# Split expert weights kept in DRAM after the first of three passes, sums kept in PSUM, and a later start for a float64 conversion

## The chip, the cores and the metric

The kernel runs on one core of one Trainium2 chip. The metric is the device time of one execution in microseconds (us), given as the median of several runs. All reading below is from one profiled execution and its trace. TensorE is PE in the profile, VectorE is DVE, ScalarE is ACT, GpSimd is POOL and SyncE is SP.

## What is computed

Three stages in a row. A delta-rule attention over 768 steps makes x (3072 tokens, 384 wide). A mixture of eight experts with Sinkhorn-balanced gates P takes x. A gated linear block with weights of type float64 takes that result.

```python
def _moe_ref(x, w_gate, w1, w2):
    P = ...                                # 8 Sinkhorn rounds on exp(x @ w_gate)
    for e in range(8):
        h = np.maximum(x @ w1[e], 0.0)     # 384 -> 1024
        out += P[:, e:e + 1] * (h @ w2[e])  # 1024 -> 384
    return out

def _moe2_ref(x, w1, w2, w3, w_out):
    h = (x @ w1) * (x @ w2) @ w3
    return h @ w_out
```

## The kernel before

Every float32 matrix product is made of three matmuls: an operand is split into a part `hi` that TensorE takes as it is and the rest `lo`, and hi·hi, hi·lo and lo·hi are summed. Splitting costs one ACT copy (`hi`) and one subtraction on POOL or DVE (`lo`).

The program is a list of operations with dependencies, priorities and estimated costs (`Plan`). Its `order` method plays them through once in the kernel's own estimates and writes out a fixed order for each engine. On the chip each engine then works through its own list strictly in that order, waiting on semaphores. An operation that is late therefore holds up all that stand behind it on its engine.

Three stretches follow each other. Up to about 530 us of the span: attention, the gates and expert 0. From there to about 1960 us, phase B: experts 1 to 7. To the end, phase C: the gated block. Phase B is 42 **units**: three passes over the tokens (two blocks of 512 in each, `PASSES`), in each pass seven experts, in each expert two halves `h` of the hidden width. A unit has 138 matmuls of 512 columns. Its first layer has 66: for each of two column **pairs** `q` (256 hidden units each), seven steps over three PSUM banks X, Y and Z, in a Strassen-like scheme with eleven block products instead of twelve or more, on sums of blocks of x (`forms`, made at each pass's start) and on sums of blocks of w1 (`wS`). Its second layer has 72 (`m2`): six sums of twelve matmuls, each read out by DVE into `tmp`, times P, and added to `acc` by POOL.

- **Weights, `load_pair`.** For each pair, four SP DMAs bring raw w1 and w2 blocks into the two `rawB` buffers. ACT copies and POOL (or DVE) subtractions make hi and lo in `wA`, five small sums on POOL or DVE make the Strassen combinations, and more copies and subtractions make `wS`. This is done for every unit, in all three passes anew, though the weights are the same. `wA` and `wS` hold two units: the weights of unit n+1 go where those of unit n-1 were, which is free when unit n-1's second layer has been read.
- **Sums, `hold` and `done`.** In steps 0, 2 and 3 of a pair ACT copies a bank to one of four SBUF buffers `rt` (`hold`). TensorE's next product into that bank waits for the copy. In steps 1, 4 and 5 `done` adds another bank to that buffer (DVE), ACT makes ReLU of it as hi, DVE makes lo; the `rt` buffer is free after the last of the three.
- **Conversion, `convert`.** The gated block's weights come as float64. 72 jobs on one buffer each (`cvr`, `cv`) turn them into hi and lo by integer operations: five DVE, two ACT and three POOL-or-DVE operations, a load and two stores on SP. They have the lowest priority and may begin when the buffers of phase B are open.
- **`add_first`.** Once in each pass, at expert 4, the result of expert 0 is read from DRAM, scaled and added. It takes two of the four `rt` buffers and both `tmp` buffers meanwhile.

Of the kernel before, what the change touches and what calls it, by code (L numbers as in the profile page):

```python
# [6 lines left out]
F32 = mybir.dt.float32  # L7
# [14 lines left out]
NE = 8  # L22
# [20 lines left out]
BB = 2.0  # L43
NG12 = 1
# [265 lines left out]
class Kernel:  # L310
# [56 lines left out]
    def setup(self):  # L367
# [22 lines left out]
                  w3_d=((2, 128, 8, 1024), F32))  # L390
# [448 lines left out]
    def load_pair(self, e_, h, q, prio):  # L839
# [4 lines left out]
        ps = 2 * h + q  # L844
        raws = []
# [29 lines left out]
        for m, src, dst, key in ((256, lambda: T["rawB"][:, r1.at, 0:256], lambda i: ws(i), lambda i: ("wS", ps, i, 0)),  # L875
                                 (256, lambda: T["rawB"][:, r2.at, 0:256], lambda i: ws(i, 256), lambda i: ("wS", ps, i, 1)),
                                 (128, lambda: T["rawB"][:, r1.at, 256:384], lambda i: self.wb(n1 + 1)[:, 768 * i:768 * i + 128], lambda i: ("w", sl2, i))):
            g.op({"ACT": actb(m)}, lambda e, src=src, dst=dst: self.copy("ACT", dst(0), src()), r=rk + ["bopen"], w=[key(0)], prio=prio)
            g.op({"POOL": pool2(m), "DVE": BB * dveb(m, True)}, lambda e, src=src, dst=dst: self.tt(e, dst(1), src(), dst(0).bitcast(F32), ALU.subtract),
                 r=rk + [key(0)], w=[key(1)], prio=prio)  # L880

# [82 lines left out]
    def unit(self, p, e_, h, pr, pe, pb):  # L964
# [22 lines left out]
        def product(q, step, idx):  # L987
# [24 lines left out]
            def done(nm, s, out):  # L1012
                t = temps[q, nm]
                tv = lambda: T["rt"][:, t.at]
                hv = lambda i: self.hv(out)[:, i]
                g.op({"DVE": dveb(512)}, lambda e: self.tt("DVE", tv(), self.ps(s, 512), tv(), ALU.add), r=[s], w=[t], prio=pe)
                g.op({"ACT": actb(512)}, lambda e: nc.scalar.activation(out=hv(0), in_=tv(), func=AF.Relu), r=[t], w=[(out, 0, 0)], prio=pe)  # L1017
                g.op({"DVE": dveb(512, True)}, lambda e: self.stt(hv(1), tv(), 0.0, hv(0).bitcast(F32), ALU.max, ALU.subtract),
                     r=[t, (out, 0, 0)], w=[(out, 1, 0)], prio=pe)
            if step == 0:  # L1020
                hold("X1", X)
            elif step == 1:
                done("X1", Z, hq["11"])
            elif step == 2:
                hold("X2", X)
            elif step == 3:
                hold("Y1", Y)
            elif step == 4:
                done("Y1", X, hq["22"])
            elif step == 5:  # L1030
                done("X2", Y, hq["12"])
            else:
                out = hq["21"]
                hv = lambda i: self.hv(out)[:, i]
                g.op({"ACT": actb(512)}, lambda e: nc.scalar.activation(out=hv(0), in_=self.ps(X, 512), func=AF.Relu),
                     r=[X], w=[(out, 0, 0)], prio=pe)
                g.op({"DVE": dveb(512)}, lambda e: self.stt(hv(1), self.ps(X, 512), 0.0, hv(0).bitcast(F32), ALU.max, ALU.subtract),
                     r=[X, (out, 0, 0)], w=[(out, 1, 0)], prio=pe)
# [50 lines left out]
    def phase_b(self):  # L1089
# [30 lines left out]
        for n, (p, e_, h) in enumerate(units):  # L1120
            pr = 400.0 + n
            if n == 0:
                for q in range(2):
                    self.load_pair(e_, h, q, 390)
# [7 lines left out]
            if n + 1 < len(units):  # L1132
                for q in range(2):
                    self.load_pair(*units[n + 1][1:], q, pr + .5)
            self.unit(p, e_, h, pr, 250.0 + n / 100, pb)
            if (e_, h) == (4, 0):
# [36 lines left out]
    def convert(self):  # L1173
# [12 lines left out]
        for nm, src, kk, c0, m in jobs:  # L1186
# [5 lines left out]
                     m * 1024, ["bopen"], [raw], pr)  # L1192
# [248 lines left out]
```

## Time and profile before

| what | value |
|---|---|
| median of 3 runs | 2313.74 us (2311.77 to 2315.23) |
| the profiled execution's own time | 2319.72 us |
| its span, first to last instruction | 2318.0 us |
| mean granted TensorE clock in the span | 0.965 of full |
| busy share of PE, DVE, POOL, ACT | 93%, 62%, 53%, 36% |
| moved by DMA | 194.82 MB, mean 84 GB/s |

The profile gives for each engine the busy time, and for each stretch of the span the busy time and the number of instructions. Idle time of an engine is put down to the engine whose semaphore ended the wait. A granted clock below 1 means that TensorE ran below its full 2.4 GHz in part of the stretch.

### The profile page before, as it was taken

The page shows a single profiled execution, that of the slowest core. Times are in us where ns is not written, and L with a number is a line of the kernel's source. Part 1 is how long each engine was busy: PE and PEld are TensorE (multiplying, and loading weights), DVE is VectorE, ACT ScalarE, POOL GpSimd, SP SyncE. Part 2 cuts the span into 40 slices and gives each one's busy share as a digit, 9 for nine tenths or more (in the row PEclk, how much of TensorE's full clock was granted, in tenths as well). Part 3 has the DMA queues.
Part 4 walks back from the last instruction along what each step waited for, and adds up shares of the span by engine and source line. Part 5 has one row for each costly group of instructions (what it writes and reads, how often), then busy time and mean ns, then how long its engine had stood idle before and what let it go on. Part 6 is the DMA issues. An engine that isn't in the chain of part 4 may idle for free.

```text
span 2318.0 us, 40182 instructions
## 1 busy us (share of the span) xinstructions
PE 2153.9 (93%) x16017; PEld 1822.8 (79%) x16017; DVE 1436.1 (62%) x2037; ACT 843.5 (36%) x1664; POOL 1233.7 (53%) x1264
## 2 busy tenths in 40 slices
PE   2999999989999799989999799999999999999999
PEld 2899999987777677767777577788887788888888
DVE  7566765667878877777787786655555555222211
ACT  3333243334434343444443334433343333122222
POOL 3000000047887987787887897876678765300000
PEclk6989999999999999999999899999999999999999
DMA  5231232133233332243233332232222214700000
GB/s 187 87 100 39 81 91 59 31 107 118 94 123 103 105 96 85 84 127 110 84 98 104 110 96 73 64 105 64 64 67 70 64 60 154 145 28 28 14 14 28
DMA packets 200476, 194.82 MB, mean 84 GB/s; under 512 B 13984, under 2 KB 175712, under 8 KB 199520
## 3 DMA queue, kind: packets, MB, share of 16 engines
q1 hardware_dynamic: 182528, 174.43, 24.4%
q0 software_dynamic: 17760, 17.83, 3.0%
q8 instruction: 125, 2.05, 0.4%
q14 instruction: 63, 0.52, 0.1%
HBM read 156.98 MB, written 35.23 MB: 83 GB/s over the span
## 4 chain that ended last, share of the span: by engine, by line
PE 55%; POOL 14%; DVE 11%; DMA 9%; issue 6%; ACT 4%; SPq 1%; DVEq 0%; POOLq 0%; ACTq 0%
PE b L332 55%; DMA rawB<-in_moe_w 3%; POOL rawB L343 3%; POOL acc L343 3%; POOL cv L343 3%; POOL wA L343 2%; DVE cv L346 2%; POOL wS L343 2%; DMA w_d<-cv 2%; SPq L363 1%; DVE hB L346 1%; DVE cv L1199 1%; DVE tmp L343 1%; DMA xst<-xs_d 1%; ACT wA L336 1%
## 5 line engine op out<-in xcount | busy, mean ns | idle before, releaser
L332 PE MATMUL b<-hB,wA 128*128 128x512 f32 x2277 | 580.1, 395 | 1.5 <-DVE hB L346 1.4
L332 PEld LDWEIGHTS b<-hB,wA 128*128 128x128 f32 x2277 | 427.3, 188 | 105.7 <-DVE hB L346 3.1
L343 POOL TENSOR_TENSOR wA<-rawB,wA 128x768 fp32r<-128x768 f32 (+2 forms) x228 | 326.2, 1439 | 171.1 <-ACT wA L336 169.1
L343 POOL TENSOR_TENSOR acc<-acc,tmp 128x512 f32<-128x512 f32 x252 | 340.0, 1351 | 67.7 <-DVE tmp L343 65.4
L343 DVE TENSOR_TENSOR rt<-b,rt 128x512 f32<-128x512 f32 x300 | 204.0, 685 | 247.5 <-PE b L332 217.4
L332 PE MATMUL b<-xr,wA 128*128 128x256 f32 (+1 forms) x1620 | 327.6, 340 | 0.0
L332 PE MATMUL b<-hA,wA 128*128 128x256 f32 (+1 forms) x1611 | 326.0, 335 | 0.8 <-DVE hA L346 0.7
L332 PEld LDWEIGHTS b<-xr,wA 128*128 128x128 f32 x1620 | 256.5, 196 | 33.7 <-DVE rt L343 0.4
L332 PEld LDWEIGHTS b<-hA,wA 128*128 128x128 f32 x1611 | 247.5, 190 | 36.3 <-DVE hA L346 3.7
L332 PE MATMUL b<-xT,wA 128*128 128x512 f32 x1008 | 251.4, 390 | 1.5 <-POOL wA L343 1.2
L332 PE MATMUL b<-xT,wS 128*128 128x512 f32 x756 | 215.0, 410 | 32.9 <-ACT rt L336 25.0
L336 ACT ACTIVATE wA<-rawB 128x768 fp32r<-128x768 f32 (+2 forms) x252 | 157.8, 627 | 228.6 <-DMA rawB<-in_moe_w 166.8
L343 DVE TENSOR_TENSOR tmp<-b,pb 128x512 f32<-128x512 f32 x234 | 159.7, 683 | 123.1 <-PE b L332 111.7
L336 ACT ACTIVATE rt<-b 128x512 f32<-128x512 f32 x300 | 174.3, 592 | 149.1 <-PE b L332 107.7
L332 PEld LDWEIGHTS b<-xT,wA 128*128 128x128 f32 x1008 | 188.9, 188 | 43.2 <-POOL wA L343 1.8
L346 DVE SCALAR_TENSOR_TENSOR hB<-rt,hB 128x512 fp32r<-128x512 f32 x170 | 169.5, 1003 | 62.6 <-ACT hB L1017 60.8
L332 PEld LDWEIGHTS b<-xT,wS 128*128 128x128 f32 x756 | 145.6, 196 | 76.2 <-ACT rt L336 33.3
L343 POOL TENSOR_TENSOR rawB<-rawB 128x128 f32<-128x128 f32 x349 | 194.5, 564 | 20.4 <-DVE rawB L343 7.1
L343 POOL TENSOR_TENSOR cv<-cv 128x256 f32<-128x256 f32 (+3 forms) x172 | 136.3, 792 | 40.2 <-DVE cv L1203 14.8
L343 POOL TENSOR_TENSOR tt<-a,bm 128x256 f32<-128x256 f32 x7 | 5.3, 757 | 267.0 <-DVE a L574 192.6
L1017 ACT ACTIVATE hB<-rt 128x512 fp32r<-128x512 f32 x170 | 105.9, 627 | 90.7 <-DVE rt L343 89.8
L343 POOL TENSOR_TENSOR wS<-rawB,wS 128x256 fp32r<-128x256 f32 x145 | 122.8, 861 | 7.6 <-ACT wS L336 5.5
(164 smaller groups left out, 2877.6 us busy)
## 6 DMA issues: line engine op xcount, KB each, us to landing
rawB<-in_moe_w SPq DMA_DIRECT2D x336, 192.0 KB, 3.2
w_d<-cv SPq DMA_DIRECT2D x112, 128.0 KB, 1.7
pb<-p_d SPq DMA_DIRECT2D x42, 256.0 KB, 3.4
cvr<-in_w3T SPq DMA_DIRECT2D x32, 256.0 KB, 3.3
wS<-w_d POOLq DMA_DIRECT2D x32, 256.0 KB, 3.5
kt<-in_kT SPq DMA_DIRECT2D x12, 512.0 KB, 5.5
qt<-in_qT SPq DMA_DIRECT2D x12, 512.0 KB, 5.1
cvr<-in_moe_w SPq DMA_DIRECT2D x24, 256.0 KB, 3.2
```

Source lines behind the costliest of these rows:

```text
L332: self.nc.tensor.matmul(*args, skip_group_check=True, **kw)
L336: self.nc.scalar.activation(out=out, in_=in_, func=AF.Copy, **({} if scale is None else {"scale": scale}))
L343: self.E[eng].tensor_tensor(out=out, in0=in0, in1=in1, op=op)
L346: self.nc.vector.scalar_tensor_tensor(out=out, in0=in0, scalar=scalar, in1=in1, op0=op0, op1=op1)
L363: return self.g.op({eng: cost}, lambda _: e.dma_start(out=out(), in_=in_()), r=r, w=w, prio=prio, nbytes=nbytes, lat=lat)
L1017: g.op({"ACT": actb(512)}, lambda e: nc.scalar.activation(out=hv(0), in_=tv(), func=AF.Relu), r=[t], w=[(out, 0, 0)], prio=pe)
L1199: g.op({"DVE": dveb(m)}, lambda e, f=f, rv=rv: ts(out=f(), in0=rv()[:, :, 1], scalar1=3, scalar2=0x3FFFFFF8, op0=ALU.logical_shift_left, o ...
```

## The change

There are three edits. In the first pass `load_pair` does as before and then also writes the finished `wA` pair (1.5 MB) and `wS` (0.5 MB) to DRAM, by SP DMAs of low priority. In the second and third pass it is only two DMAs on POOL's queue that read them back. Second, `done` no longer adds into the `rt` buffer: DVE reads a bank and the buffer and writes the sum to a PSUM bank (Z in steps 1 and 4, Y in step 5), and ReLU and remainder are then made from that bank, so that `rt` is free after the addition. Third, the conversion's loads wait for the accumulator of unit 11 (`NC0`), that is for the end of the first pass but two units.

```diff
-                  w3_d=((2, 128, 8, 1024), F32))
+                  w3_d=((2, 128, 8, 1024), F32),
+                  wq_d=((NE, 4, 128, 3072), F32), ws_d=((NE, 4, 128, 1024), F32))
...
-    def load_pair(self, e_, h, q, prio):
+    def load_pair(self, p, e_, h, q, prio):
...
+        wk = lambda n: [("w", n % 8, i) for i in range(2)]
+        sk = [("wS", ps, i, m) for i in range(2) for m in range(2)]
+        two = lambda: T["wA"][:, n1 % 8:n1 % 8 + 2].rearrange("p a n -> p (a n)")
+        if p:
+            self.dma(two, lambda: T["wq_d"][e_, ps], 1572864, [("wq", e_, ps)], wk(n1) + wk(n1 + 1), prio, eng="POOL")
+            self.dma(lambda: T["wS"][:, ps], lambda: T["ws_d"][e_, ps], 524288, [("ws", e_, ps)], sk, prio, eng="POOL")
+            return
...
+        self.dma(lambda: T["wq_d"][e_, ps], lambda: two().bitcast(F32), 1572864, wk(n1) + wk(n1 + 1), [("wq", e_, ps)], 1000)
+        self.dma(lambda: T["ws_d"][e_, ps], lambda: T["wS"][:, ps].bitcast(F32), 524288, sk, [("ws", e_, ps)], 1000)
...
+            def relu(s, out):
+                hv = lambda i: self.hv(out)[:, i]
+                g.op({"ACT": actb(512)}, lambda e: nc.scalar.activation(out=hv(0), in_=self.ps(s, 512), func=AF.Relu),
+                     r=[s], w=[(out, 0, 0)], prio=pe)
+                g.op({"DVE": dveb(512)}, lambda e: self.stt(hv(1), self.ps(s, 512), 0.0, hv(0).bitcast(F32), ALU.max, ALU.subtract),
+                     r=[s, (out, 0, 0)], w=[(out, 1, 0)], prio=pe)
+
-            def done(nm, s, out):
+            def done(nm, s, out, dst):
                 t = temps[q, nm]
...
+                g.op({"DVE": dveb(512)}, lambda e: self.tt("DVE", self.ps(dst, 512), self.ps(s, 512), T["rt"][:, t.at], ALU.add),
+                     r=[s, t], w=[dst], prio=pe)
+                relu(dst, out)
...
-                done("X1", Z, hq["11"])
+                done("X1", Z, hq["11"], Z)
...
-                done("Y1", X, hq["22"])
+                done("Y1", X, hq["22"], Z)
...
-                done("X2", Y, hq["12"])
+                done("X2", Y, hq["12"], Y)
...
+            if n == NC0:
+                self.after("cv0", [g.wr["acc", 0, 2]], 2)
...
-                     m * 1024, ["bopen"], [raw], pr)
+                     m * 1024, ["bopen", "cv0"], [raw], pr)
```

The written-out order changes on every engine. First POOL, in an ordinary unit in the middle of the second pass. Before, the rows on `rawB`, `wA` and `wS` are the splitting of the next unit's weights, those on `cv` the conversion, those on `acc` the sums:

```order
L343 TENSOR_TENSOR acc<-acc,tmp 128x512
L343 TENSOR_TENSOR wA<-rawB,wA 128x768
L343 TENSOR_TENSOR wA<-rawB,wA 128x640
L343 TENSOR_TENSOR cv<-cv 128x256
L343 TENSOR_TENSOR rawB<-rawB 128x128
L343 TENSOR_TENSOR cv<-cv 128x256
L343 TENSOR_TENSOR rawB<-rawB 128x128 x4
L343 TENSOR_TENSOR cv<-cv 128x256
L343 TENSOR_TENSOR wS<-rawB,wS 128x256 x2
L343 TENSOR_TENSOR wA<-rawB,wA 128x128
```

After the change, one such unit on POOL, with what each row waits for:

```order
L364 DMA wA<-wq_d 128x3072 [waits DMASW7_49,PE_49]
L344 TENSOR_TENSOR acc<-acc,tmp 128x512 [waits DVE_49]
L364 DMA wA<-wq_d 128x3072 [waits DMASW0_49,PE_49]
L344 TENSOR_TENSOR cv<-cv 128x256 [waits DVE_49]
L344 TENSOR_TENSOR cv<-cv 128x256 [waits Activation_49]
L364 DMA wS<-ws_d 128x1024 [waits DMASW1_49,PE_49]
L364 DMA wS<-ws_d 128x1024 [waits DMASW2_49,PE_49]
L344 TENSOR_TENSOR cv<-cv 128x256 [waits DVE_49,Activation_49]
L344 TENSOR_TENSOR cv<-cv 128x256 [waits Pool_49]
L344 TENSOR_TENSOR acc<-acc,tmp 128x512 [waits DVE_49]
L344 TENSOR_TENSOR cv<-cv 128x256 [waits Activation_49]
```

The splitting rows are gone; four DMA issues stand in their place, each behind a wait for PE, and conversion rows now follow each other closely. Next ACT at the seam between two units of the second pass, before: `rt<-b` is the hold on which TensorE waits, `cv<-cv` the conversion's hi copy:

```order
L1205 ACTIVATE cv<-cvr 128x256
L336 ACTIVATE cv<-cv 128x256
L336 ACTIVATE wA<-rawB 128x768
L336 ACTIVATE rt<-b_132 128x512
L336 ACTIVATE wA<-rawB 128x640
L1205 ACTIVATE cv<-cvr 128x256
L336 ACTIVATE rt<-b_127 128x512
L1017 ACTIVATE hA<-rt 128x512
```

and at such a seam after the change:

```order
L337 ACTIVATE rt<-b_132 128x512
L337 ACTIVATE cv<-cv 128x256
L1217 ACTIVATE cv<-cvr 128x256
L337 ACTIVATE cv<-cv 128x256
L1217 ACTIVATE cv<-cvr 128x256
L337 ACTIVATE cv<-cv 128x256
L337 ACTIVATE rt<-b_129 128x512
L1025 ACTIVATE hB<-b_133 128x512
```

The raw copies have left; the conversion's copies still stand ahead of a hold, and ReLU (`hB`) now reads a bank. Last, SP in the first pass after the change, where the new stores stand among the raw loads of the next pair:

```order
L364 DMA wq_d<-wA 128x3072
L364 DMA rawB<-in_moe_w 128x3x128
L364 DMA rawB<-in_moe_w 128x384
L364 DMA rawB<-in_moe_w 128x3x128
L364 DMA rawB<-in_moe_w 128x384
L364 DMA ws_d<-wS 128x1024
```

Before, SP has only the four `rawB` rows of these. The large store comes behind the next pair's loads, the small one ahead of the pair after that.

## Rows read from the trace of the kernel before

**Rows 1.** The page: busy time of the engines over the span, and in 40 equal slices of it the busy tenths of PE and the granted clock of TensorE in tenths.

```profile
PE 2153.9 (93%) x16017; PEld 1822.8 (79%) x16017; DVE 1436.1 (62%) x2037; ACT 843.5 (36%) x1664; POOL 1233.7 (53%) x1264
...
PE   2999999989999799989999799999999999999999
...
PEclk6989999999999999999999899999999999999999
```

**Rows 2.** Stretches of the span: start and end, length, then busy time and number of instructions of PE, of its weight loads, of DVE, ACT and POOL, then the granted clock, the DMA engines' busy share and GB/s.

```profile
550.00:1425.00 875.00, 799.26 (x3339) 632.61 (x3338) 678.34 (x942) 354.74 (x726) 728.25 (x754) 0.97 0.32 100
1425.00:1950.00 525.00, 517.34 (x2226) 418.89 (x2225) 298.30 (x376) 210.83 (x399) 383.79 (x389) 0.99 0.24 72
1525.00:1740.00 215.00, 215.00 (x936) 175.25 (x935) 117.03 (x154) 89.44 (x169) 146.49 (x158) 1.00 0.24 73
575.00:600.00 25.00, 19.84 (x82) 15.47 (x82) 21.62 (x26) 8.14 (x18) 21.54 (x21) 0.97 0.29 91
750.00:825.00 75.00, 60.02 (x242) 46.97 (x241) 61.56 (x78) 25.55 (x53) 67.93 (x64) 0.91 0.34 102
975.00:1050.00 75.00, 66.25 (x265) 50.63 (x263) 57.58 (x75) 32.80 (x65) 64.19 (x64) 0.95 0.39 121
1225.00:1300.00 75.00, 58.10 (x229) 46.03 (x228) 59.62 (x78) 25.47 (x54) 63.48 (x62) 0.86 0.34 108
1500.00:1525.00 25.00, 22.90 (x93) 18.17 (x92) 20.46 (x20) 7.34 (x16) 24.13 (x19) 0.93 0.36 103
1750.00:1800.00 50.00, 45.61 (x191) 36.26 (x190) 32.40 (x38) 19.52 (x38) 44.01 (x41) 0.97 0.22 64
1950.00:1975.00 25.00, 25.00 (x112) 20.61 (x111) 13.60 (x17) 5.71 (x8) 10.29 (x11) 1.00 0.68 240
```

**Rows 3.** The same stretches 550 to 1425 and 1425 to 1950 us, but busy time and number of the instructions on the conversion's tile `cv` alone, of DVE, ACT and POOL.

```profile
550.00:1425.00 875.00, 291.49 (x388) 56.02 (x137) 129.28 (x164) 0.97 0.32 100
1425.00:1950.00 525.00, 0.00 (x0) 0.00 (x0) 0.00 (x0) 0.99 0.24 72
```

**Rows 4.** Likewise for the instructions on the raw weights' tile `rawB`, that is the splitting of weights, of DVE, ACT and POOL.

```profile
550.00:1425.00 875.00, 57.44 (x68) 124.20 (x243) 377.58 (x419) 0.97 0.32 100
```

**Rows 5.** What PE waited for: us in total, times, longest. The first row is of 550 to 1425 us, the second of 1425 to 1950 us.

```profile
PE b L332 <- ACT rt L336: 68.2, 31, 11.3
...
PE b L332 <- ACT rt L336: 5.4, 4, 3.2
```

**Rows 6.** The timeline of PE at six of these waits: start, length, instruction, and in brackets the idle time before it and who ended it.

```profile
592.45 1.65 PE L332 MATMUL b<-xT,wS 128*128 128x512 f32 x6 [1.94 <-ACT rt L336]
...
598.72 1.65 PE L332 MATMUL b<-xr,wS 128*128 128x512 f32 x3 [3.22 <-ACT rt L336]
...
779.79 1.65 PE L332 MATMUL b<-xr,wS 128*128 128x512 f32 x3 [10.03 <-ACT rt L336]
...
1277.83 1.65 PE L332 MATMUL b<-xT,wS 128*128 128x512 f32 x6 [1.42 <-ACT rt L336]
...
1292.90 1.65 PE L332 MATMUL b<-xr,wS 128*128 128x512 f32 x3 [11.34 <-ACT rt L336]
...
1396.55 0.97 PE L332 MATMUL b<-xr,wS 128*128 128x512 f32 x3 [0.72 <-ACT rt L336]
```

**Rows 7.** The timeline of ACT ahead of another of PE's waits (TensorE stood from 1237.8 to 1241.95 us).

```profile
1240.27 0.42 ACT L336 ACTIVATE cv<-cv 128x256 fp32r<-128x256 f32 x1 [6.78 <-DVE cv L346]
1240.59 0.83 ACT L336 ACTIVATE wA<-rawB 128x768 fp32r<-128x768 f32 x1
1241.32 0.58 ACT L336 ACTIVATE rt<-b 128x512 f32<-128x512 f32 x1
```

**Rows 8.** What ACT waited for: the first row is of 550 to 1425 us, the second and third of 1525 to 1740 us.

```profile
ACT rt L336 <- DVE hA L346: 30.1, 14, 5.9
...
ACT wA L336 <- DMA rawB<-in_moe_w: 27.0, 17, 5.4
ACT wA L336 <- PE b L332: 26.3, 3, 9.6
```

**Rows 9.** Groups of instructions from 530 to 1930 us: number, busy time in us, mean ns of one, then idle time before them.

```profile
L343 POOL TENSOR_TENSOR acc<-acc,tmp 128x512 f32<-128x512 f32 x240 | 324.5, 1354 | 53.8 <-DVE tmp L343 51.5
...
L343 DVE TENSOR_TENSOR rt<-b,rt 128x512 f32<-128x512 f32 x243 | 164.6, 683 | 60.6 <-PE b L332 30.4 <-ACT rt L336 28.4 <-ACT wA L336 0.5
L346 DVE SCALAR_TENSOR_TENSOR hB<-rt,hB 128x512 fp32r<-128x512 f32 x162 | 163.4, 1015 | 60.2 <-ACT hB L1017 58.5
...
L346 DVE SCALAR_TENSOR_TENSOR hB<-b,hB 128x512 fp32r<-128x512 f32 x81 | 53.1, 678 | 5.0 <-ACT hB L1035 5.0
```

**Rows 10.** DMAs. Four rows of the page's list: number, KB of each, median us from issue to landing. Then the issue times in ns (shortest, median, longest) of two loads on POOL's queue at 1953 to 1957 us, the landing times (shortest, median, longest) of the four loads on that queue from 1940 to 1970 us, and that of one 768 KB store on SP at 1023.9 us.

```profile
rawB<-in_moe_w SPq DMA_DIRECT2D x336, 192.0 KB, 3.2
...
xT<-w_d POOLq DMA_DIRECT2D x4, 1536.0 KB, 10.2
...
xf_d<-acc SPq DMA_DIRECT2D x4, 768.0 KB, 6.3
wA<-wo_d POOLq DMA_DIRECT2D x2, 1536.0 KB, 6.7
...
L363 POOL DMA_DIRECT2D xT<-w_d x2: 531/536/541, 1953.6 to 1957.0; - x2
...
DMA to landing us min/median/max: 3.4/9.9/10.9
...
DMA to landing us min/median/max: 3.2/3.2/3.2
```

More of the change, by code (lines that the diff above doesn't have):

```diff
@@ L43 @@
 BB = 2.0
+NC0 = 11
 NG12 = 1
@@ L1010, in hold @@
                 g.op({"ACT": actb(512)}, lambda e: self.copy("ACT", T["rt"][:, t.at], self.ps(s, 512)), r=[s], w=[t], prio=pe)
-            def done(nm, s, out):
-                t = temps[q, nm]
[L1014 to L1019, printed above, removed]
+            def relu(s, out):
[5 more added lines that the diff above has]
+            def done(nm, s, out, dst):
+                t = temps[q, nm]
+                g.op({"DVE": dveb(512)}, lambda e: self.tt("DVE", self.ps(dst, 512), self.ps(s, 512), T["rt"][:, t.at], ALU.add),
+                     r=[s, t], w=[dst], prio=pe)
+                relu(dst, out)
             if step == 0:
@@ L1028, in product @@
             elif step == 4:
-                done("Y1", X, hq["22"])
+                done("Y1", X, hq["22"], Z)
             elif step == 5:
-                done("X2", Y, hq["12"])
+                done("X2", Y, hq["12"], Y)
             else:
[L1033 to L1038, printed above, removed]
+                relu(X, hq["21"])
         for idx, (q, step) in enumerate(self.STEPS):
@@ L1123, in phase_b @@
                 for q in range(2):
-                    self.load_pair(e_, h, q, 390)
+                    self.load_pair(p, e_, h, q, 390)
             if (e_, h) == (1, 0):
@@ L1133, in phase_b @@
                 for q in range(2):
-                    self.load_pair(*units[n + 1][1:], q, pr + .5)
+                    self.load_pair(*units[n + 1], q, pr + .5)
             self.unit(p, e_, h, pr, 250.0 + n / 100, pb)
+            if n == NC0:
+                self.after("cv0", [g.wr["acc", 0, 2]], 2)
             if (e_, h) == (4, 0):
```

## The prediction, on record before the changed kernel ran

> **What bounds the kernel now.** I read the page's totals and slices first. TensorE is busy 93% of the span, and of the 40 slices the first and those from 9 to 23 show it idle in part, the 23rd with the clock at 8 tenths [rows 1]. So only time in which TensorE stands, or runs at a lower clock, can be won.
>
> Then the stretches of phase B. From 1525 to 1740 us TensorE is busy 215.00 of 215 us at clock 1.00 with 936 matmuls: 215 / 936 = 0.2297 us each, 138 x 0.2297 = 31.7 us for a unit. This is the floor, which the change does not touch. From 550 to 1425 us there are 3339 matmuls, which at the floor need 767.0 us: 875 - 767.0 = 108.0 us are lost, 75.7 of them idle and the rest at a lower clock. From 1425 to 1950 us, 525 - 2226 x 0.2297 = 13.7 us are lost [rows 2]. Phase B loses 121.7 us, and that is the ceiling of a gain.
>
> The two stretches do the same units and the same splitting of weights. What differs is the conversion: DVE spends 291.5 us on it in the first and nothing in the second, POOL 129.3 us and ACT 56.0 us [rows 3]. With it POOL is busy 83% and DVE 78%, without it 73% and 57% [rows 2].
>
> The waits tell the path. Of the idle 75.7 us, 68.2 are TensorE waiting for the ACT copy of a bank to `rt`, in 31 waits; in the later stretch it is 5.4 us in 4 [rows 5]. I followed ACT back from each wait over 0.3 us to its last own idle time, and found three main kinds [rows 6]:
> - ACT stood in front of a conversion copy whose DVE or POOL operand was late, and the hold stood behind it. 8 waits, 1.94 us at 592.45 to 1.42 us at 1277.83, together 19.1 us. One of them in full: ACT idle 6.78 us before `cv`, then a raw copy, then the hold [rows 7].
> - ACT stood in front of a ReLU whose DVE sum was late. 9 waits, 3.22 us at 598.72 to 0.72 us at 1396.55, together 16.0 us.
> - No free `rt` buffer, because DVE had not made the remainder: 10.03 us at 779.79 and 11.34 us at 1292.90, both while `add_first` holds two of the four buffers. ACT waits for DVE in this way 30.1 us in all [rows 8].
>
> Waits behind a late raw load make up 11 us, the rest is small.
>
> **The change part by part.**
>
> *Splitting.* It takes POOL 377.6, ACT 124.2 and DVE 57.4 us of the 875 [rows 4]. In passes two and three all of it goes. POOL without it would be busy 728.3 - 377.6 = 351 us; four issues of about 0.54 us in each of 27.6 units add 60 us. That is 47%, where it was 83%. DVE falls from 78% to 71%, ACT from 41% to 26%.
>
> *Sums in PSUM.* The remainder on two SBUF operands takes 1015 ns, on a bank and one SBUF operand 678 ns; six of eight in a unit change over, 2.0 us less for DVE in a unit and no competition with POOL there. The addition takes 683 ns into SBUF [rows 9]. A DVE write to PSUM is not in the trace: below, I see no reason for less than 678 ns; above, twice the 683 ns, 4.1 us of DVE in a unit, which its idle share of 43% without a conversion covers. I take 683, the nearest row. The `rt` buffer comes free after the addition instead of two operations later, which bears on the third kind of wait. Bank Z is held longer, about 0.68 + 0.6 + 0.68 us after step 4 [rows 7, 9], but its next user is the next unit's first layer, behind 72 matmuls or 16.5 us: nothing.
>
> *Later conversion.* Twelve units run with splitting but without conversion. That is what 1425 to 1950 us shows. The same work (388 DVE instructions there, 399 in the changed order) then lies in units 12 to 39 beside almost no splitting. In the changed order the conversion's copies still stand ahead of holds on ACT.
>
> *Loads.* 4 MB in a unit of 31.7 us are 132 GB/s. From 1950 to 1975 us the queues moved 240 GB/s with TensorE busy 25.00 of 25 us [rows 2]. A 1.5 MB load on POOL's queue lands after 6.7 to 10.9 us [rows 10]. Both `wA` loads start when unit n-1's second layer has been read, and are wanted one unit later: 2 x 10.9 = 21.8 us at the worst of these rows, 9.9 us to spare. The `wS` loads may start half a unit earlier. On POOL only the last sum of unit n-1 stands behind the first load's wait, and it needs the same matmuls. I cost the loads at nothing; without the cover each microsecond late costs 28 us, one for each unit.
>
> The Trainium skill (SBUF — State Buffer, SBUF: two separate sides) speaks against issuing them from POOL: DVE operations in a two-port mode keep GpSimd from writing the descriptors, and the transfer stands still meanwhile; SP or ACT should issue. The issues here took 531 to 541 ns beside a DVE busy 13.6 of 25 us [rows 2, 10], so the trace shows no such stall, but with little conversion-like work beside them. By the rule each load could start later by one DVE operation, which the spare time covers, and the sum would be the same; it decides only as part of the second rival.
>
> *Stores.* 56 in the first pass. A 768 KB store takes 3.2 us undisturbed [rows 10], so 1.5 MB at most 6.4 us and 0.5 MB at most 3.2. The large one stands behind the next pair's raw loads, with half a unit to finish; the small one delays loads by up to 3.2 us. The split weights have time: in the clean stretch ACT waits up to 9.6 us for TensorE to free their place [rows 8]. Nothing; 56 / 2 x 3.2 = 90 us if that cover were gone.
>
> *What remains lost:*
> - First pass without conversion: `add_first` as at 1750 to 1800 us, 50 - 191 x 0.2297 = 6.1, and half of the start's 25 - 82 x 0.2297 = 6.2: 9 us.
> - Units 12 and 13 with both kinds of work: in 550 to 1425 us the ordinary units lose 108.0 less the three special stretches of 19.4, 14.1 and 22.4 (750, 975 and 1225 us), 52.1 us in the other 650 us, which hold 18.9 units at the floor, 2.8 us each: 6 us.
> - Seam of passes one and two: 3.6 us without conversion (1500 us), 14.1 with it (975 us); 7, between.
> - Ordinary units with conversion in passes two and three. The first two kinds of wait, 35.1 us, with their share of clock 35.1 x 108.0 / 75.7 = 50 us. Bounds 0 and 50; I take 0.4 of it, since POOL's load nearly halves but DVE's and the order on ACT change little: 20 us.
> - Two `add_first`: 6.1 each without conversion, up to 22.4 with it; buffers free earlier, 5 each: 10 us.
> - Seam of passes two and three, as the first one without splitting: 5 us.
>
> Together 57 us [rows 2, 5]. The gain is 121.7 - 57 = 65 us: 2319.7 becomes 2255 us for the profiled execution. That execution lies 6.0 us above the median of 2313.7, so for the median 2249 us.
>
> **The rivals.**
>
> *The waits move with the conversion.* If late conversion steps come from its own chain and its place on ACT, not from the load beside it, units 12 to 39 lose what units 0 to 25 lost: 108.0 x 399 / 388 = 111, and the clean rest, 14 units at the 13.7 us in 16.1 units of the later stretch, 12 more. That is 123 for 121.7: no change, 2314 us, and up to 2325 if the denser conversion rows on POOL add 0.4 us a unit. It decides once a unit with conversion loses 4 us. For it: the copies ahead of holds in the new order. Against it: the third kind of wait and the raw loads are not the conversion's, and DVE steps lengthen beside POOL's.
>
> *Weights land late.* One `wA` load of over 20 us, or both in a row over 31.7 us. At 4 us late in 28 units 112 us are lost: 2249 + 112 = 2361 us; it is slower than before from 2.4 us on. Only the loads' doubling over the longest row would do it.
>
> *Stores bind the first pass.* A third of the 90 us: 2278 us.
>
> *Nearly all is won.* The third kind of wait vanishes and conversion hides: 9 + 2 + 4 + 0 + 6 + 4 = 25 us remain, 2217 us.
>
> **How the numbers follow.** The forecast, 2230 to 2265 us, has 0.58; nearly all won 0.15; stores or a similar small loss (2265 to 2300) 0.12; waits that move along 0.09, half of it within 0.2%; late weights 0.06. I predict 2249 us. The range takes in nearly all won and the small loss, 2213 to 2295. A measurement can tell about 0.2%, 4.6 us, from no change. Faster by more: 0.58 + 0.15 + 0.12 = 0.85, and 0.01 of the third; same 0.04; slower 0.10.
>
> **What would show it.** In the profile after: no conversion before about 900 us; `rawB` rows only in the first pass; units of 31.7 us between 560 and 900 us; PE's waits for `rt` down from 73.6 to about 25 us, the ones at `add_first` under 5 us each; POOL under 55% busy in passes two and three; the remainder on a bank at 0.68 us. Waits of PE for `wA` or `wS` landed by DMA would show the second rival, PE waits of the first kind at their old size the first one. The prediction is wrong if the first pass is not clean without the conversion, or if passes two and three lose over 2 us a unit.

## The result, and the profile after

The changed kernel takes 2225.93 us (median of 4 runs, 2215.08 to 2229.92) where the kernel before takes 2314.48 us on the same chip: 0.9611 of its time, 95% interval 0.9576 to 0.9646. That is 88.5 us less; 65 were forecast, with a whole range of 2213 to 2295 us.

The page of the profiled execution (2226.69 us, span 2224.9 us), first the busy times, the slices of PE and of its clock, as in [rows 1]; then two groups of VectorE and three of DMA issues (count, KB each, median us to landing):

```profile
PE 2130.1 (96%) x16017; PEld 1819.0 (82%) x16017; DVE 1245.0 (56%) x1958; ACT 720.6 (32%) x1384; POOL 832.2 (37%) x895
...
PE   3999999989999999999999999999999999999999
...
PEclk6889999999999999999999999999999999999999
...
L344 DVE TENSOR_TENSOR b<-b,rt 128x512 f32<-128x512 f32 x252 | 174.2, 696 | 111.2 <-ACT rt L337 66.8
...
L347 DVE SCALAR_TENSOR_TENSOR hB<-b,hB 128x512 fp32r<-128x512 f32 x253 | 172.5, 687 | 49.5 <-ACT hB L1025 48.2
...
wA<-wq_d POOLq DMA_DIRECT2D x56, 1536.0 KB, 8.9
wq_d<-wA SPq DMA_DIRECT2D x28, 1536.0 KB, 7.2
wS<-ws_d POOLq DMA_DIRECT2D x56, 512.0 KB, 5.0
```

PE's holes in slices 14, 18 and 23 are gone; slice 9, which lies before phase B, shows 8 tenths as before. The addition into a bank takes 696 ns (683 was taken), the remainder on a bank 687 ns where it was 1015 on two SBUF operands [rows 9]. Stretches, with the columns of [rows 2]:

```profile
530.00:960.00 430.00, 420.33 (x1801) 337.53 (x1799) 223.25 (x314) 169.73 (x326) 297.59 (x320) 1.00 0.58 202
960.00:1360.00 400.00, 396.83 (x1710) 322.32 (x1711) 262.66 (x444) 124.23 (x240) 197.75 (x222) 1.00 0.57 195
1360.00:1780.00 420.00, 412.85 (x1776) 335.38 (x1775) 283.67 (x458) 136.09 (x259) 206.13 (x223) 0.99 0.56 193
```

The conversion now runs from 920 to 1785 us. In the second pass POOL is busy 197.75 of 400 us, 49%, and VectorE 262.66, 66%; before, in the stretch with conversion, they were busy 83% and 78% [rows 2]. PE's waits from 550 to 1425 us, which answer to [rows 5] (us, times, longest):

```profile
PE b L333 <- DVE hA L347: 7.4, 2, 3.9
PE b L333 <- ACT rt L337: 6.9, 6, 2.2
```

Before the change the waits for `rt` were 68.2 us in 31, the longest 11.3 us.

A table of all kernels is the shortest way to say where time went. It is worked out from the traces: the end of VectorE's reading of the sixth second-layer sum closes a unit, and so the column "unit 0" is when that unit ends, the next three are how long units 1 to 13, 14 to 27 and 28 to 41 take (the rest of pass one, pass two, pass three), and "rest" is what follows. At 31.7 us a unit the three would take 412, 444 and 444 us. P stands for the sums in PSUM, W for the stored weights, C for the late conversion.

| kernel | ratio to before | unit 0 | pass 1 | pass 2 | pass 3 | rest |
|---|---|---|---|---|---|---|
| before | 1 | 555.3 | 462.9 | 505.4 | 450.6 | 343.7 |
| P, W and C (the change) | 0.961 | 546.4 | 432.6 | 453.1 | 450.4 | 342.4 |
| C | 1.006 | 539.4 | 427.9 | 506.0 | 500.1 | 342.2 |
| P | 0.978 | 542.8 | 452.4 | 471.2 | 445.4 | 341.1 |
| W | 0.976 | 542.0 | 457.1 | 452.2 | 458.2 | 342.5 |
| W and C | 0.972 | 545.2 | 449.0 | 450.4 | 456.7 | 341.8 |
| P and W | 0.973 | 542.1 | 460.7 | 453.8 | 446.6 | 341.2 |
| P and C | 0.975 | 536.6 | 422.7 | 468.5 | 473.3 | 342.0 |
| change + work on POOL | 0.987 | 540.2 | 431.2 | 485.5 | 479.8 | 341.8 |
| change + half of that work | 0.975 | 550.3 | 431.4 | 485.1 | 449.9 | 343.5 |
| loads twice | 1.005 | 540.9 | 425.3 | 469.3 | 454.2 | 432.7 |
| loads twice, order kept | 0.988 | 542.1 | 434.2 | 491.7 | 475.1 | 344.1 |
| stores twice | 0.981 | 539.0 | 471.5 | 454.5 | 451.4 | 341.4 |
| loads on SP | 0.955 | 541.8 | 426.7 | 449.0 | 445.1 | 342.6 |

Of the 93.1 us between the two spans, 52.3 are pass two, 30.3 pass one, 0.2 pass three, 8.9 the time before unit 0 ends and 1.3 the rest. The change and the four kernels that add work only to its later passes have the same operations in the same order up to unit 13, and end unit 0 at 540 to 550 us: differences below 10 us before it are no effect of an edit. Their units 1 to 12 together take 393.6 to 394.3 us. Unit 13, where their orders part, takes 31.7 to 40.1 us, and so their first pass takes 425 to 434 us. The profiled execution of C is its fastest, 10 us below its median, that with half of the work its slowest, 10.5 us above.

### The profile page after: what moved, and what is told of

It is laid out like the page before. It is cut to its first block, busy times and chain, and to the rows that moved or that the text cites. A ratio compares the mean times of both kernels' runs of the same rounds, so it can differ in the third digit from the quotient of the medians.

```text
span 2224.9 us, 39081 instructions
## 1 busy us (share of the span) xinstructions
PE 2130.1 (96%) x16017; PEld 1819.0 (82%) x16017; DVE 1245.0 (56%) x1958; ACT 720.6 (32%) x1384; POOL 832.2 (37%) x895
## 4 chain that ended last, share of the span: by engine, by line
PE 82%; DVE 6%; DMA 5%; POOL 3%; issue 2%; ACT 2%; SPq 0%; POOLq 0%; DVEq 0%; ACTq 0%
PE b L333 82%; DMA rawB<-in_moe_w 2%; DMA xs_d<-xst 1%; DMA xst<-xs_d 1%; DVE prod L344 1%; POOL rawB L344 1%; POOL wA L344 1%; DMA w_d<-cv 0%; POOL wS L364 0%; DVE cv L347 0%; DVE b L344 0%; POOL wS L344 0%; DMA wA<-wq_d 0%; SPq L364 0%; POOL acc L344 0%
## 5 line engine op out<-in xcount | busy, mean ns | idle before, releaser
L344 DVE TENSOR_TENSOR b<-b,rt 128x512 f32<-128x512 f32 x252 | 174.2, 696 | 111.2 <-ACT rt L337 66.8
L333 PE MATMUL b<-xT,wS 128*128 128x512 f32 x756 | 202.9, 394 | 7.6 <-ACT rt L337 5.1
L344 POOL TENSOR_TENSOR cv<-cv 128x256 f32<-128x256 f32 (+2 forms) x177 | 129.1, 729 | 192.3 <-DVE cv L1215 113.0
L347 DVE SCALAR_TENSOR_TENSOR hB<-b,hB 128x512 fp32r<-128x512 f32 x253 | 172.5, 687 | 49.5 <-ACT hB L1025 48.2
L1025 ACT ACTIVATE hB<-b 128x512 fp32r<-128x512 f32 x253 | 150.0, 597 | 121.7 <-DVE b L344 96.1
L344 POOL TENSOR_TENSOR wA<-rawB,wA 128x768 fp32r<-128x768 f32 (+2 forms) x73 | 101.8, 1400 | 91.9 <-ACT wA L337 91.1
L344 DVE TENSOR_TENSOR rt<-b,rt 128x512 f32<-128x512 f32 x48 | 33.2, 692 | 179.3 <-PE b L333 179.3
L347 DVE SCALAR_TENSOR_TENSOR hA<-b,hA 128x512 fp32r<-128x512 f32 x131 | 90.3, 689 | 48.3 <-ACT hA L1025 28.1
L337 ACT ACTIVATE cv<-cv 128x256 fp32r<-128x256 f32 x72 | 29.1, 404 | 269.2 <-DVE cv L347 269.2
L333 PE MATMUL b<-wS,xT 128*128 128x512 f32 x432 | 101.6, 396 | 2.9 <-ACT wS L337 1.6
```

The costliest lines, as they stand in the source:

```text
L333: self.nc.tensor.matmul(*args, skip_group_check=True, **kw)
L337: self.nc.scalar.activation(out=out, in_=in_, func=AF.Copy, **({} if scale is None else {"scale": scale}))
L344: self.E[eng].tensor_tensor(out=out, in0=in0, in1=in1, op=op)
L347: self.nc.vector.scalar_tensor_tensor(out=out, in0=in0, scalar=scalar, in1=in1, op0=op0, op1=op1)
```

## Experiments: each part of the change, alone and left out

**The change without the sums in PSUM (W and C).** `done` adds into `rt` again, and ReLU and remainder are made from there:

```diff
...
-                g.op({"DVE": dveb(512)}, lambda e: self.tt("DVE", self.ps(dst, 512), self.ps(s, 512), T["rt"][:, t.at], ALU.add),
-                     r=[s, t], w=[dst], prio=pe)
-                relu(dst, out)
+                g.op({"DVE": dveb(512)}, lambda e: self.tt("DVE", tv(), self.ps(s, 512), tv(), ALU.add), r=[s], w=[t], prio=pe)
...
```

> The changed kernel with the sums in the rt buffers as before; stored weights and late conversion stay. Theory L (the load of splitting on POOL, DVE and ACT beside the conversion made the waits): nearly all of the gain stays, 2230 to 2250 us, with PE waits for rt of some 10 us, most of them at add_first where two rt buffers are taken. Theory R (the rt buffers and the remainder on two SBUF operands made the waits): most of the gain goes, 2275 us or more.

2243.77 us, 0.9718 (0.9689 to 0.9746), as theory L had it. Against the change pass one loses 16.4 us and pass three 6.3; the second pass loses nothing. Pass one, with splitting and stores but hardly any conversion, is thus where the sums in PSUM are worth most once W and C are there.

**The change with the conversion from the start (P and W).**

```diff
-                     m * 1024, ["bopen", "cv0"], [raw], pr)
+                     m * 1024, ["bopen"], [raw], pr)
```

> The changed kernel with the conversion free to begin when phase B's buffers are open, as before. Theory L: the conversion falls into the first pass beside the splitting, which loses there what units 0 to 13 of the kernel before lost in part (about 45 us less what the sums in PSUM save), and the rest stays clean: 2245 to 2265 us. Theory R: the first pass is clean too, 2220 to 2235 us.

2247.67 us, 0.9728 (0.9703 to 0.9754), as theory L had it. Pass one is back at 460.7 us, as before the change. The two later passes keep their gain.

**The change with the weights split anew in each pass (P and C).**

```diff
-        if p:
+        if False:
...
-        self.dma(lambda: T["wq_d"][e_, ps], lambda: two().bitcast(F32), 1572864, wk(n1) + wk(n1 + 1), [("wq", e_, ps)], 1000)
-        self.dma(lambda: T["ws_d"][e_, ps], lambda: T["wS"][:, ps].bitcast(F32), 524288, sk, [("ws", e_, ps)], 1000)
...
```

> The changed kernel without stores and read-back: weights are split anew in every pass, the conversion still begins at unit 11 and the sums stay in PSUM. Theory L: units 12 to 39 have splitting and conversion together as in the kernel before, 1.5 to 2.8 us lost in each: 2265 to 2300 us. Theory R: 2225 to 2245 us.

2248.84 us, 0.9745 (0.9713 to 0.9777), better than theory L and worse than theory R had it. Passes two and three take 24.5 and 29.3 us more than the floor's 444 each. Pass one, here without stores, is the shortest of all, 422.7 us.

**The kernel before with the sums in PSUM alone (P).** The first edit of this section the other way round:

```diff
-                done("X1", Z, hq["11"])
+                done("X1", Z, hq["11"], Z)
...
```

> The kernel before with the sums in PSUM alone. Theory L: the waits for a free rt buffer go (21 us and their share of clock, some 30 us) and little else: 2275 to 2300 us. Theory R: 2225 to 2255 us.

2259.72 us, 0.9779 (0.9754 to 0.9804), between the two ranges: P alone is worth about 51 us, 34 of them in pass two. The waits for a free `rt`, the prediction's third kind, vanish, and those behind a late conversion copy, its first kind, nearly do: 0.9 us in one wait, where they were 19.1 in 8. POOL is still busy 83% of pass two. What is left from 550 to 1885 us, followed back in the same way, is 24.8 us behind a late VectorE sum, more than before, and 13.1 behind a late raw load.

**The kernel before with the stored weights alone (W).** `load_pair` as in the change, the rest as before:

```diff
+        if p:
+            self.dma(two, lambda: T["wq_d"][e_, ps], 1572864, [("wq", e_, ps)], wk(n1) + wk(n1 + 1), prio, eng="POOL")
...
+        self.dma(lambda: T["wq_d"][e_, ps], lambda: two().bitcast(F32), 1572864, wk(n1) + wk(n1 + 1), [("wq", e_, ps)], 1000)
...
```

> The kernel before with stored and read-back weights alone: conversion from the start of phase B, sums in the rt buffers. If each edit relieves only its own units, passes two and three become clean (units 14 to 25 at 2.8 us, the seam of 14 and the add_first of 22 us, about 60 us with the loss of the third pass) and the first pass keeps its 50 us: 2255 to 2270 us. If the sums in PSUM are what removes the waits, units 14 to 25 keep theirs and 2285 us or more remain.

2257.56 us, 0.9755 (0.9731 to 0.9778), as the first theory had it. Pass two falls from 505.4 to 452.2 us, pass one hardly; pass three grows by 7.6 us, for which no run has the cause.

**The kernel before with the late conversion alone (C).**

```diff
+NC0 = 11
...
+            if n == NC0:
+                self.after("cv0", [g.wr["acc", 0, 2]], 2)
...
-                     m * 1024, ["bopen"], [raw], pr)
+                     m * 1024, ["bopen", "cv0"], [raw], pr)
```

> The kernel before with the conversion begun at unit 11 alone. If the waits move along with the conversion (the first rival of the prediction, here undiluted): 2305 to 2325 us. If beginning later thins the conversion out or spares the start: 2285 to 2305 us.

2327.4 us, 1.0057 (1.0036 to 1.0078): slower by 0.6%, 2 us beyond the first theory's range. Its three passes, columns as above:

```profile
540.00:965.00 425.00, 414.67 (x1784) 334.90 (x1783) 249.20 (x321) 171.06 (x324) 314.60 (x320) 1.00 0.22 67
965.00:1470.00 505.00, 467.75 (x1950) 369.31 (x1949) 392.52 (x545) 207.58 (x422) 408.01 (x430) 0.97 0.32 99
1470.00:1970.00 500.00, 459.65 (x1909) 362.63 (x1908) 359.14 (x485) 194.24 (x390) 386.80 (x404) 0.97 0.34 106
```

PE stands 10 us in the first and 37 and 40 in the others. Pass one gains 35.0 us and pass three loses 49.5. This is the prediction's first rival, undiluted: where splitting and conversion meet and the sums are in `rt`, a unit loses 4 us on the mean of a pass, wherever that is.

So the parts work by place. C clears pass one and would hand the loss to pass three; W clears the passes into which C hands it. P takes off part of the loss where both kinds of work remain (34 us of pass two, alone) and little where W has been: P and W are worth 51 and 58 us alone, and 63 together. The ten ordinary units of pass two (15 to 20 and 23 to 26, without seams and `add_first`) show it by themselves: together they lose 30.2 us before the change, 15.9 with P, 0.7 with W, 12.7 with P and C, and 0.8 with the change.

## Experiments: what in the splitting did the harm, and what the DMAs cost

**The change with dummy work on POOL.** In passes two and three POOL makes ten subtractions a pair, of the splitting's sizes, which nothing reads; no raw loads, no ACT copies and no splitting on VectorE come back.

```diff
+            r1, r2 = self.rawB.new(), self.rawB.new()
+            for m in (768, 640, 128, 128, 128, 128, 128, 256, 256, 128):
+                g.op({"POOL": pool2(m)}, lambda e, m=m: self.tt(e, T["rawB"][:, r2.at, 0:m], T["rawB"][:, r2.at, 0:m], T["rawB"][:, r1.at, 0:m], ALU.subtract),
+                     r=[(r1, 0)], w=[(r2, 0)], prio=prio)
             return
```

> The changed kernel with ten POOL subtractions on the raw-weight buffers for each pair in passes two and three, of the sizes that splitting has (768, 640, 5 x 128, 2 x 256, 128 columns), whose results nothing reads. No raw loads, no ACT copies. If POOL's load makes the conversion late, it loses as splitting anew did: 2240 to 2260 us. If the raw loads and ACT copies were what mattered: 2222 to 2234 us.

2286.56 us, 0.9870 (0.9846 to 0.9895), 61 us more than the change: more than either theory had, and more than splitting anew costs, which may hand POOL's part to VectorE. The ordinary units of pass two lose 18.9 us. PE's waits for a hold from 550 to 1885 us, 10.6 us in the change, are:

```profile
PE b L333 <- ACT rt L337: 40.9, 24, 6.1
```

Followed back as in the prediction, 36.6 us of them stand behind a late VectorE sum, the prediction's second kind, and 2.1 behind a late conversion copy, its first.

**Half of that work.**

```diff
-            for m in (768, 640, 128, 128, 128, 128, 128, 256, 256, 128):
+            for m in (768, 256, 128, 128, 128):
```

> The changed kernel with half of the dummy subtractions on GpSimd that cost 61 us before (1408 instead of 2688 elements per partition and pair of chunks in passes 2 and 3; nothing reads their results). Theory 'in proportion': half the loss, 2248 to 2265 us. Rival 'a queue that overflows': nothing is lost while GpSimd has slack within a unit: 2222 to 2238 us.

2251.55 us, 0.9745 (0.9716 to 0.9774), in the range of 'in proportion'. Some half of the loss, 26 us, but not by halves of each unit: the written order lets these operations run ahead, and the last of them starts at 1400 us. Stretches of it, in the second pass and then in the third:

```profile
960.00:1160.00 200.00, 191.82 (x815) 153.23 (x816) 153.53 (x213) 59.55 (x117) 187.17 (x222) 0.99 0.58 199
1160.00:1360.00 200.00, 188.90 (x788) 151.54 (x787) 162.20 (x220) 54.29 (x109) 184.81 (x213) 0.97 0.48 166
...
1560.00:1760.00 200.00, 196.09 (x843) 158.64 (x842) 137.83 (x223) 62.24 (x120) 110.99 (x118) 0.99 0.55 191
```

and of the kernel with the full work:

```profile
960.00:1160.00 200.00, 188.15 (x792) 150.22 (x791) 155.04 (x210) 58.62 (x114) 180.34 (x223) 0.97 0.56 195
1360.00:1560.00 200.00, 190.18 (x810) 152.37 (x809) 162.93 (x219) 60.18 (x119) 184.83 (x225) 0.99 0.53 184
```

With POOL busy 90 to 94%, pass two takes 485 us in both; with POOL at 55%, pass three of the second kernel is as short as that of the change (449.9 and 450.4 us). So more work on POOL, with no raw load and no ACT copy, brings waits back. VectorE is busier with it, 77 to 81% of these stretches where the change has 66%: its steps last longer, and the order hands it POOL's part of the conversion (455 conversion instructions with the full work, 399 in the change). These two were not tried apart. How the waits reach PE is seen in VectorE's groups from 965 to 1400 us, first the change, then the kernel with half the work (busy us, mean ns):

```profile
L344 DVE TENSOR_TENSOR b<-b,rt 128x512 f32<-128x512 f32 x80 | 55.1, 694 | 30.3 <-ACT rt L337 21.8 <-PE b L333 7.9
...
L347 DVE SCALAR_TENSOR_TENSOR cv<-cvr,cv 128x256 int32<-128x256 int32 x31 | 20.3, 654 | 0.4
```

```profile
L344 DVE TENSOR_TENSOR b<-b,rt 128x512 f32<-128x512 f32 x74 | 50.8, 691 | 16.4 <-PE b L333 8.3 <-ACT rt L337 7.7
L347 DVE SCALAR_TENSOR_TENSOR cv<-cvr,cv 128x256 int32<-128x256 int32 x29 | 35.4, 1221 | 0.5
```

A conversion step on two SBUF operands goes from 654 to 1221 ns beside a busy POOL, the addition on a bank stays at 0.69 us. VectorE's sums, behind those steps in its list, come late, and so do ACT's ReLU and the hold behind it. The Trainium skill (SBUF — State Buffer, SBUF: two separate sides) says that a VectorE operation with two SBUF inputs and a GpSimd operation that reads SBUF share one pair of ports, which the one that starts first keeps for its whole instruction. The rows agree: the step with two SBUF inputs lengthens, the addition with one does not. How much of the 61 us comes this way, how much from the steps handed to VectorE and how much from POOL's own lateness, the runs do not separate.

**The loads made twice**, each 1.5 MB load issued a second time into the same place:

```diff
+            self.dma(two, lambda: T["wq_d"][e_, ps], 1572864, [("wq", e_, ps)], wk(n1) + wk(n1 + 1), prio, eng="POOL")
             return
```

> The changed kernel with each 1.5 MB weight load of passes two and three issued twice, so 7 MB in a unit of 31.8 us. If the loads have the spare time that I worked out, the doubled ones (four of about 9 us each) just fill it: 2226 to 2250 us. If loads are close to late already, each unit waits for several us: over 2300 us.

2326.17 us, 1.0045 (1.0024 to 1.0065), in the second theory's range, but for neither theory's reason. One stretch and PE's longest wait:

```profile
965.00:1650.00 685.00, 670.22 (x2867) 542.47 (x2866) 390.52 (x649) 202.56 (x386) 309.63 (x365) 0.99 0.75 277
```

```profile
PE b L333 <- DMA wS<-w_d: 85.5, 1, 85.5
```

At 277 GB/s most units still take 31.8 us, and no wait of PE for a weight load is listed: the weights were not late. But the order counts all transfers in one queue of its own estimates and had put the conversion off (67 of its 387 VectorE instructions start after the last unit, none in the change), and the gated block stood 85.5 us for converted weights. So the run was made again with the second load counted as one byte and issued ahead of the `wS` load, which keeps the conversion among the units:

```diff
+            self.dma(two, lambda: T["wq_d"][e_, ps], 1, [("wq", e_, ps)], wk(n1) + wk(n1 + 1), prio, eng="POOL")
```

> The changed kernel with every 1.5 MB load of split weights in passes 2 and 3 issued twice, as in the run before (2326 us), but the planner that writes the order out is told that the second one moves one byte, so the conversion keeps its place among the units and ends with unit 38 or so. Theory 'spare time': the loads have 9.9 us to spare per unit and a second 1.5 MB (6.7 us alone) still fits: 2222 to 2245 us, units of passes 2 and 3 at 31.8 us, the loss of the run before was the conversion written behind the last unit. Rival 'transfers compete': the loads or the conversion's own transfers come late: over 2270 us, with TensorE waiting in the units of passes 2 and 3.

2286.16 us, 0.9881 (0.9856 to 0.9905), in the rival's range: passes two and three lose 63 us against the change. What VectorE and POOL waited for from 965 to 1400 us:

```profile
DVE cv L1212 <- DMA w_d<-cv: 58.8, 17, 7.5
```

```profile
POOL wA L364 <- DMA wA<-wq_d: 58.1, 18, 7.3
```

In the change the first of these is 13.7 us. Weights were late to PE only 10.3 us in 3 waits. What grew is the wait of VectorE for the conversion's stores, which land later (3.3 us, 2.3 in the change), and that of POOL, which stands for the first load before it issues the second into the same buffer. The second of these comes from the way the loads were doubled; which of the two makes more of the loss was not tried apart. The spare time of the weights is confirmed but for those 10.3 us; that the DMA queues have as much to spare is not.

**The stores made twice**, to a second place in DRAM:

```diff
...
+        self.dma(lambda: T["wq2_d"][e_, ps], lambda: two().bitcast(F32), 1572864, wk(n1) + wk(n1 + 1), [("wq2", e_, ps)], 1000)
+        self.dma(lambda: T["ws2_d"][e_, ps], lambda: T["wS"][:, ps].bitcast(F32), 524288, sk, [("ws2", e_, ps)], 1000)
```

> The changed kernel with every store of split weights in the first pass made twice (1.5 MB and 0.5 MB per pair of chunks, to a second place in DRAM): 58.7 MB more to write between 500 and 960 us. Theory 'stores cost nothing' (the prediction's): 2222 to 2240 us. Rival 'the store holds its weight buffer' (the prediction's 2278 case): a buffer is not free until its stores have ended, 7.2 us more per pair, so units of the first pass grow past 33 us and the time is 2245 to 2290 us.

2267.99 us, 0.9814 (0.9770 to 0.9857): the rival's size. The first pass, and the waits of PE in it:

```profile
545.00:960.00 415.00, 388.75 (x1601) 302.23 (x1602) 187.54 (x275) 149.84 (x285) 263.76 (x283) 0.98 0.80 296
```

```profile
PE b L333 <- ACT wS L337: 9.8, 10, 1.5
PE b L333 <- ACT wA L337: 8.5, 6, 3.9
PE b L333 <- POOL wA L344: 6.7, 6, 1.2
```

Pass one grows from 425–434 to 471.5 us: split weights come late. Whether they wait for the stores of the place they go to, as the rival had it, or for raw loads that stand behind stores on SP, is not shown. In units 1 to 12, almost all ahead of the conversion, one set of stores costs 9.5 us (384.5 us without them in P and C, 393.6 to 394.3 with), the second 37 (430.8). Without the sums in PSUM the first set costs more: pass one takes 427.9 us with C and 449.0 with W and C. So the prediction's "nothing" for the stores does not hold, and twice the stores are past the edge.

**The loads issued from SP.**

```diff
-            self.dma(two, lambda: T["wq_d"][e_, ps], 1572864, [("wq", e_, ps)], wk(n1) + wk(n1 + 1), prio, eng="POOL")
+            self.dma(lambda: two().bitcast(F32), lambda: T["wq_d"][e_, ps], 1572864, [("wq", e_, ps)], wk(n1) + wk(n1 + 1), prio)
...
```

> The changed kernel with the 112 loads of split weights issued from SyncE instead of GpSimd. Theory 'the queue does not matter': 2215 to 2236 us; the Trainium skill's page on SBUF, in its part on the port that VectorE and GpSimd share, has a rule that transfers issued by GpSimd can be starved while VectorE works; if it bites here the time falls by up to the 0.6 to 2 us that GpSimd-released waits cost around 1250 and 1700 us. Rival 'in-order issue': a load that waits for its buffer holds up the conversion's and the sums' transfers behind it on SyncE: 2240 to 2300 us.

2206.61 us, 0.9545 (0.9522 to 0.9567): faster than the change, whose interval begins at 0.9576, and the best kernel here. Both theories had it slower than that. Its busy times and the landing of the loads, then its second pass:

```profile
PE 2117.3 (96%) x16017; PEld 1807.3 (82%) x16017; DVE 1221.8 (55%) x1932; ACT 720.2 (33%) x1384; POOL 797.9 (36%) x809
...
wA<-wq_d SPq DMA_DIRECT2D x56, 1536.0 KB, 8.6
```

```profile
960.00:1360.00 400.00, 397.11 (x1722) 322.55 (x1721) 259.62 (x439) 126.64 (x247) 180.31 (x183) 1.00 0.56 199
```

The loads land hardly earlier than in the change (8.6 and 8.9 us). The Trainium skill (SBUF — State Buffer, SBUF: two separate sides) gives starved descriptors as the reason for issuing from SP or ACT; these landing times show none, so something else was won. Each of the three passes gains 4 to 6 us, mostly at the seams, where the change looks like this: VectorE, POOL and PE around 955 us.

```profile
954.54 0.68 DVE L347 SCALAR_TENSOR_TENSOR hB<-b,hB 128x512 fp32r<-128x512 f32 x1
955.14 4.95 DVE L344 TENSOR_TENSOR xr<-xT,xr 128x512 fp32r<-128x512 f32 x1
960.02 0.68 DVE L347 SCALAR_TENSOR_TENSOR hA<-b,hA 128x512 fp32r<-128x512 f32 x1
```

```profile
954.54 1.31 POOL L344 TENSOR_TENSOR xT<-rt,xT 128x512 fp32r<-128x512 f32 x1
955.80 1.30 POOL L344 TENSOR_TENSOR rt<-xT 128x512 f32<-128x512 f32 x1
957.07 2.47 POOL L344 TENSOR_TENSOR xT<-xT 128x512 fp32r<-128x512 f32 x2
959.50 0.57 POOL L364 DMA_DIRECT2D wS<-ws_d  x1
```

```profile
956.19 0.62 PE L333 MATMUL b<-hA,wA 128*128 128x512 f32 x2
960.75 0.72 PE L333 MATMUL b<-hA,wA 128*128 128x512 f32 x1 [3.94 <-DVE hA L347]
```

One subtraction of 512 columns on two SBUF operands takes 4.95 us while four POOL operations run back to back, the remainder behind it is late, and PE stands 3.94 us. Without the four load issues a unit on POOL, the order puts this subtraction of the first seam on POOL, and PE has no such wait. With the loads doubled, in the first of the two runs, they are still on POOL's queue, but there too the order puts this subtraction on POOL, and unit 13 takes 31.7 us where the change takes 38.7: at this seam its place seems to make the difference, not the queue. In the change POOL also stands before its `wS` loads, from 965 to 1400 us for:

```profile
POOL wS L364 <- PE b L333: 67.2, 25, 9.1
```

and what is behind such a load in its list waits too. Which of the two makes more of the rest of the 15 us that the three passes gain was not tried apart.

## Why the prediction was right, and what was mis-sized

The main steps of its mechanism held: the loss of phase B lay where splitting and conversion meet, C moved the conversion out of pass one, and W kept it from costing the same in the passes where it went. In size it was too careful: 2225.93 us lies below the forecast's 2230 to 2265, to which it gave 0.58, and inside the whole range by what it kept for "nearly all is won" at 0.15. The floor of 31.7 us stands. What remains lost, in its own terms, from the unit times of the change (a unit's time less 31.7):

| term | forecast | measured |
|---|---|---|
| first pass: `add_first` and start, units 12–13, seam 1→2 | 9 + 6 + 7 = 22 | 20.5 - 0.7 given back in unit 14 = 19.8 |
| ordinary units with conversion, passes 2 and 3 | 20 | 0.9 |
| two `add_first` | 10 | 3.8 + 6.5 = 10.3 |
| seam 2→3 | 5 | 5.4 |
| together | 57 | 36.4 |

One term failed: the ordinary units. The step took 0.4 of 50 us because "POOL's load nearly halves but DVE's and the order on ACT change little". The copies do stand ahead of holds, and VectorE is still busy 66% (71% was worked out), but with POOL at 49% none of PE's waits for a hold stands behind one. The lower bound, 0, was the value, and W alone reaches it in pass two, with the sums still in `rt`: 0.7 us lost in ten ordinary units. With the dummy work on POOL it is 18.9 us again. It is not the only condition, though: P alone halves the loss of these units with POOL still busy 83%. The 50 were too high besides, since 14.3 of the 35.1 us behind them lie in the three special stretches that other terms hold (the waits at 766.01, 816.27, 989.52, 1027.70, 1241.95 and 1277.83 us). Those 19 us and the 9 us before unit 0's end, which no term covered and no edit made, are all but the whole of the difference between the profiled executions' 93 us and the 65 forecast; by the medians it is 88.5. As far as the runs tell, the 9 us are chance.

The 19.8 us for the 22 of the first pass are near by luck, for two errors cancel: units 12 and 13 with the seam lost 7.2 us where 13 were forecast, and units 1 to 6 and 9 to 11 lost 6.0 us where 3 were forecast for the start. The stores, costed at nothing, account for the second: without them, in P and C, units 1 to 12 are 9.5 us shorter. The loads too were costed at nothing. The weights were not late, but with the same loads on SP the three passes are 15 us shorter: the order places other work differently, and POOL does not stand before `wS` loads, 67.2 us in the change, where the prediction looked only at what stands behind the first `wA` load.

The signs: the conversion begins at 920 us (about 900 said); PE's waits for `rt` from 550 to 1885 us are 10.6 us (about 25 said); those at `add_first` are 1.97 and 2.25 us in the first pass (under 5 each); POOL 49% (under 55). Units of the first pass before 900 us take 31.7 to 33.2 us, not all 31.7, apart from the first of them (34.7) and the two of `add_first` (39.9 and 30.2).

The rivals. Waits that move with the conversion are real: C alone is that case, 0.6% slower than before, and the forecast stood because W and P came with it. Either would have done for its range: P and C without W take 2248.84 us, W and C without P 2243.77. Weights landing late did not occur even with the loads doubled, but for 10.3 us in one of the two runs. Stores that bind the first pass appear at twice the stores, and a little of it, 9.5 us, at once. "Nearly all is won", 25 us left and 0.15, was the nearest.

## What to carry to other kernels

An engine that is off the critical path can still set the time by how full it is: with dummy work that kept POOL 90 to 94% busy a unit of the changed kernel cost some 2 us more on the mean of pass two, at 50% its ordinary units cost almost nothing. Load is not all of it: with the sums in PSUM alone about half of these units' loss was gone with POOL still at 83%. Work that is moved out of one stage costs the same in the next unless what it met there is gone as well, so price an edit in the stage into which it moves work, and together with the edits that clear that stage. When an experiment changes a list that a planner orders, look where the order put everything else before reading its total.

## What the runs showed of the hardware

Single VectorE instructions on two SBUF operands were drawn out to 4.95 and 6.13 us at the seams (0.68 us at their shortest for the same shape) beside POOL operations that followed each other closely. VectorE's addition with its result in PSUM took 696 ns, against 683 in SBUF. With the loads doubled the DMA queues moved 277 GB/s for 685 us while most units kept 31.8 us.
